# Attention with one exponential for two of four heads over a double bank, five single banks, another order of tile steps, and GpSimd's block sums in four pieces

## The chip, the core and the metric

The kernel runs on one core of a Trainium2 chip. The metric is the time of one execution on the device in microseconds (us). Below, PE is TensorE, ACT is ScalarE, DVE is VectorE, POOL is GpSimd and SP is SyncE, which issues most of the DMAs.

## The reference

x is 2048 rows by 576. The kernel computes attention with 32 heads of 18 columns on the layer norm of x and adds x, then a gated GELU block of width 4608 on the layer norm of that, and adds again:

```python
qkv = (layernorm(x) @ wqkv) ...            # q, k, v: 32 heads, 18 columns each
scores = einsum("bhqd,bhkd->bhqk", q, k) * 18 ** -0.5
p = softmax(scores, axis=-1)
h = x + (einsum("bhqk,bhkd->bhqd", p, v) ...) @ wo
g, u = layernorm(h) @ w_gate, layernorm(h) @ w_up
out = h + (gelu(g) * u) @ w_down
```

## The kernel before

The kernel has three stages: projections (to about 215 us), attention (to about 1405 us), and the gated block (to the end). The change is in attention, and in the buffers that the projections share with it.

Attention works in 32 **rounds** (n, line 1220), NS = NG x NB: eight groups of four heads, four blocks of 512 queries each. A round has 16 **key tiles** (kt) of 128 keys. In a key tile, for each of the four heads, `score` (L663) multiplies 128 keys by 512 queries into a PSUM bank, and ScalarE takes the exponential into one of four buffers `pes`. q and k stand as three stacked fp16 parts in 54 rows, and two rows more subtract the row maximum inside the product; they come from the tile `mT`. Heads 0 and 2 use partitions 0 to 63, heads 1 and 3 partitions 64 to 127. `weigh` (L673) multiplies the exponentials of the tile before with v, in two halves of 256 queries and four 32-row outputs, in fp32, into one bank `acc` (singles[3]); a column of ones gives the denominators.

The row maxima are computed ahead, one and a half rounds before they are used, by a generator `maxima` (L742): 64 units a round, each (`max_bank`, L611) a product of 128 queries by 512 keys and a VectorE reduction (L629). For one head in four a pair of units is joined: ScalarE takes a Relu of a difference ("over", L623) and VectorE adds the other product and reduces (both, L627). After the 64 units `max_finish` (L635) reduces the parts on VectorE (L638), splits the result on GpSimd (L641 to L643), turns it with a DMA (L645) and loads eight rows of the next round's Q with four DMAs (L651), in the order of the heads. It falls at key tile 8 of a round and serves the next.

PSUM has eight banks: singles[0] to [3] and quads[0] to [3]. In attention, scores and maxima take the next of seven banks in turn (`m_ring`, L1216); the eighth is `acc`. In the projections products rotate over the four quads (`p_ring`).

The order within a key tile is a string (L1217), one for even and one for odd tiles: "s" a head's score and exponential, "m" a unit of the maxima, "w" half of the weighing of the tile before, "f" filler work.

```python
STEPS = ("ssmsmmfwmsw", "mssmssmfwwm")
```

`out_block` (L686) finishes a round during the next. VectorE copies the sums out of `acc` (L692, behind the last "w" of key tile 0), SyncE spreads the denominators (L695), and, after key tile 3, GpSimd inverts them (L702 to L706) and two DMAs spread them over the rows (L710, L711). After key tile 5 GpSimd multiplies, casts and takes the difference (L715 to L717), 512 columns each, and SyncE stores the two parts into X (L730). In the last two rounds VectorE does this.

TensorE, ScalarE, VectorE and GpSimd run their instructions in the order in which the code issues them. SyncE's queue is ordered by the scheduler, and is the same list before and after. In each group's first round, SyncE also carries the loads of the next group's heads (L572, L573, L593) and of the key differences (L606, L608).

Of the kernel before, what the change touches and what calls it, by code (L numbers as in the profile page):

```python
# [12 lines left out]
F32 = mybir.dt.float32  # L13
# [5 lines left out]
P = 128  # L19
# [12 lines left out]
def tile_block(  # L32
# [41 lines left out]
    singles = [ps.tile([P, 512], F32, name=f"bank{i}") for i in range(4)]  # L74
    pairs_in = ExitStack()
    psp = pairs_in.enter_context(tc.tile_pool(name="psp", bufs=1, space=bass.MemoryType.PSUM))
    quads = [psp.tile([P, 512], F32, name=f"quad{i}") for i in range(4)]

    def ring(items):
        while True:  # L80
            yield from items

    p_ring = ring(quads)
    m_ring = ring(singles)
    

# [336 lines left out]
    def idle_products(n):  # L423

        for _ in range(n):
            nc.tensor.matmul(quads[0], id16, parts[0][:, :512], start=True, stop=True)

    def turned(t0):

        cols = slice(t0 * P, (t0 + 2) * P)  # L430
        pts = [quads[1], quads[2], next(m_ring), next(m_ring)]
        for pt, c0 in zip(pts, (0, 2, NK + 1, NK + 3)):
            for c in range(2):
                for t in range(2):
                    o = (2 * c + t) * P
                    nc.tensor.matmul(pt[:, o : o + P], parts[t0 + t][:, (c0 + c) * P : (c0 + c + 1) * P],
                                     id16, start=True, stop=True)
            copy = nc.scalar.copy if c0 < NK else nc.vector.tensor_copy
            copy(XT[:, c0 : c0 + 2, cols], pt.rearrange("p (c t) -> p c t", c=2))
        pt = next(m_ring)  # L440
        for t in range(2):
            nc.tensor.matmul(pt[:, t * P : (t + 1) * P], parts[t0 + t][:, NK * P : (NK + 1) * P],
                             id16, start=True, stop=True)
        nc.scalar.copy(XT[:, NK, cols], pt[:, : 2 * P])
# [209 lines left out]
    NPE = 4  # L654
# [5 lines left out]
    ohl = view(nat1, O0 + 12 * TB, (2, TB), F16)  # L660
    rc_dram = [dram.tile([P, TPB * 4], F32, name=f"rc{i}") for i in range(2)]

    def score(n, kt, hh):  # L663

        g, qc = divmod(n, NB)
        pS = next(m_ring)
        Q, K = sets[g % 2][hh // 2]
        r = half(hh % 2, R1 + 2)
        nc.tensor.matmul(pS[:, :TB], K[r, kt * P : (kt + 1) * P],  # L669
                         Q[r, qc * TB : (qc + 1) * TB], start=True, stop=True)  # L670
        nc.scalar.activation(pes[(2 * kt + hh // 2) % NPE][:, hh % 2], pS[:, :TB], AF.Exp, scale=ex_reg)  # L671

    def weigh(n, kt, acc):  # L673
        for q in range(2):
# [11 lines left out]
    def out_block(n, acc):  # L686

        g, qc = divmod(n, NB)  # L690
        oT = oTs[n % 2]
        (nc.scalar.copy if n >= NS - 2 else nc.vector.tensor_copy)(oT, acc[:, :TB])  # L692
        R = 4 * TB // P
        rc = small.tile([P, R], F32, tag="rc", name="rc")
        (nc.scalar if n == NS - 1 else nc.sync).dma_start(rc, oT.rearrange("(h c) q -> h c q", c=32)[:, DH].rearrange(  # L695
            "h (p q) -> h p q", q=R))
        yield
        if n < NS - NB:
            den, rc = rc, small.tile([P, R], F32, tag="rp", name="rp")
            re = small.tile([P, R], F32, tag="re", name="re")  # L700
            for c in range(0, R, 4):
                nc.gpsimd.tensor_tensor(rc[:, c : c + 4], den[:, c : c + 4],  # L702
                                        minus_one.to_broadcast([P, 4]), op=ALU.pow)
            nc.gpsimd.tensor_mul(re, den, rc)
            nc.gpsimd.tensor_scalar(re, re, -1.0, 2.0, op0=ALU.mult, op1=ALU.add)
            nc.gpsimd.tensor_mul(rc, rc, re)  # L706
        else:
            nc.vector.reciprocal(rc, rc)
        rd = rc_dram[n % 2]
        nc.sync.dma_start(rd, rc)  # L710
        nc.sync.dma_start(rcb, rd.rearrange("(h p) q -> h (p q)", h=4).unsqueeze(1)  # L711
                         .to_broadcast([4, 32, TB]))
        yield
        if n < NS - 2:
            nc.gpsimd.tensor_mul(oT, oT, rcb)  # L715
            nc.gpsimd.tensor_copy(ohl[:, 0], oT)
            nc.gpsimd.tensor_sub(ohl[:, 1], oT, ohl[:, 0])  # L717
        else:
            nc.vector.tensor_mul(oT, oT, rcb)
            (nc.scalar.copy if n == NS - 1 else nc.vector.tensor_copy)(ohl[:, 0], oT)  # L720
            nc.vector.tensor_sub(ohl[:, 1], oT, ohl[:, 0])
        sl = slice(qc * TB, (qc + 1) * TB)
        for hh in range(4):
            f, end = (4 * g + hh) * DH, (4 * g + hh + 1) * DH
            r = 32 * hh
            while f < end:
                c, p = divmod(f, P)
                k = min(end - f, P - p)
                if c < NK:
                    nc.sync.dma_start(XT[p : p + k, c : c + NK + 2 : NK + 1, sl], ohl[r : r + k])  # L730
                else:
                    other = nc.gpsimd if n >= NS - 2 else nc.sync
                    nc.sync.dma_start(XT[p : p + k, NK, sl], ohl[r : r + k, 0])
                    other.dma_start(XT[TAIL + p : TAIL + p + k, NK, sl], ohl[r : r + k, 1])
                f += k
                r += k
# [5 lines left out]
    def maxima():  # L742

        for n in range(NS):
            mx = small.tile([P, TPB, 4, NB], F32, tag="mx", name="mx")
            over, both = ("over", "both") if n else ("one", "one")
            if n:
                nc.gpsimd.memset(mx[:, :, 0, 1::2], LOWEST)
            for u in range(0, UPS, 2):
                t, k = divmod(u, NB)  # L750
                for unit in (("one", t, k, 1), (over, t, k + 1, 0), ("one", t, k + 1, 1), ("one", t, k, 2),
                             ("one", t, k, 3), (both, t, k, 0), ("one", t, k + 1, 2), ("one", t, k + 1, 3)):
                    max_bank(n, mx, *unit)
                    yield
            max_finish(n, mx)
# [458 lines left out]
        take(mxs, 3 + (i % 5 == 4))  # L1214
        take(fill, 2 + (i % 5 in (1, 3)))
    m_ring = ring(singles[:3] + quads)  # L1216
    STEPS = ("ssmsmmfwmsw", "mssmssmfwwm")  # L1217
    OUT_AT = STEPS[0].rindex("w")
    prev = None
    for n in range(NS):  # L1220
        g, qc = divmod(n, NB)
        acc = singles[3]
        late = n > NS - NB
        for kt in range(NT):
            heads = iter(range(4))
            halves = weigh(*prev) if prev is not None else iter(())
            for step_no, step in enumerate(STEPS[kt % 2]):
                if step == "s":
                    score(n, kt, next(heads))
                elif step == "m":  # L1230
                    take(mxs)
                elif step == "w":
                    take(halves)
                    if kt == 0 and step_no == OUT_AT and prev is not None:
                        ob = out_block(prev[0], prev[2])
                        next(ob)
                else:
                    if n < NS - 1 or kt < 11:
                        take(fill, 2)
                    take(side)  # L1240
            prev = (n, kt, acc)
            if n and kt in ((1 if n == NS - 1 else 3, 6) if late else (3, 5)):
                take(ob)
            if late and kt == 11:
                run(fill)
                fill = wo_block(qc - 1, m_ring)
                take(fill, qc == 3)
            if n == NS - 2 and kt == NT - 1:
                rows = rows0()
            if n * NT + kt >= (NS - 1) * NT - 1:  # L1250
                take(rows, 2)
            if g == 0 and qc == 0 and kt == NT - 1:
                run(fill)
                init_set(sets[1])
            if g + 1 < NG and kt == 2 and qc == (1 if g == 0 and NB > 1 else 0):
                load_stacks(g + 1)
                load_ends(g + 1)
            if g + 1 < NG and kt == 8 and qc == (1 if g == 0 and NB > 1 else 0):
                key_steps(g + 1)
            if n == 1 and kt == 8:  # L1260
                load_w(of, wo, nc.gpsimd)
            if n == 2 and kt == 4:
                side = prepare_wo()
            if n == NS - NB and kt == 2:
                blank_rows()
                load_matrix(w_gate, 0, nc.gpsimd)
            if n == NS - NB and kt == 8:
                side = chain(split_early(0, 0, lambda: load_matrix(w_up, 0, nc.gpsimd)), pause(2),
                             split_early(0, 1, lambda: load_matrix(w_gate, 1, nc.gpsimd)),
                             pause(2), until_ready(second))  # L1270
# [106 lines left out]
```

## Time and profile before

| | us |
|---|---|
| median of 3 runs | 2634.18 (2632.51 to 2635.2) |
| profiled execution, its own time | 2638.2 |
| its span, first to last instruction | 2636.4 |
| PE busy over the span | 2589.5 (98%) |
| DVE | 2014.7 (76%) |
| ACT | 1662.0 (63%) |
| POOL | 819.3 (31%) |
| exponentials (L671), 2048 | 655.4 + 504.8 |
| weighing products (L677), 8192 records | 608.3 |
| maximum reductions (L629), 1552 | 552.6 + 478.6 |
| granted TensorE clock, mean | 0.997 |

Busy time counts an instruction from its start to its modelled end; instructions of one engine overlap at their ends, so that an engine that is busy all the time can still start one earlier or later. The shares are means over three stages with different limits, and attention is read from its own windows. Each fp32 product of the weighing has two records. In the timelines, rows show start, length, engine, line, operation, output and input, and how many instructions are merged; in brackets stands the idle time before and what ended it. "SPq" is the time of issue of a DMA, not its landing.

### The profile page before, as it was taken

How to read it: one execution, taken by the hardware profiler on the slowest of the kernel's cores; microseconds unless marked ns; L12 is line 12 of the kernel's file. 1: busy time of each engine (PE TensorE's matmuls, PEld its weight loads, DVE VectorE, ACT ScalarE, POOL GpSimd, SP SyncE). 2: the span in 40 equal slices, each digit the busy share in tenths (PEclk: the TensorE clock that was granted, in tenths of full speed). 3: DMA queues.
4: the chain of work that ended last, by engine and by line, in shares of the span. 5: the costliest groups of instructions: out<-in, count | busy, mean ns of one | idle time of the engine just before them, and what ended most of it. 6: DMA issues, size and time to landing. Idle time of an engine off the chain costs nothing.

```text
span 2636.4 us, 53635 instructions
## 1 busy us (share of the span) xinstructions
PE 2589.5 (98%) x20765; PEld 1200.4 (46%) x20765; DVE 2014.7 (76%) x3886; ACT 1662.0 (63%) x3122; POOL 819.3 (31%) x1160
## 2 busy tenths in 40 slices
PE   8899999999999999999999999999999999999999
PEld 4443333333333333333345555555555555555555
DVE  7368999999999999999866765656565656566653
ACT  5217999999999999999775433333333333333332
POOL 4201452232323232324575432222222222222221
PEclk9999999999999999999999999999999999999999
DMA  7411110101101010101125410101010101011110
GB/s 216 98 50 54 43 43 19 42 16 31 33 16 45 16 44 16 44 18 31 29 55 126 81 39 30 34 30 34 30 34 30 33 30 33 30 32 32 31 57 36
DMA packets 169137, 114.69 MB, mean 44 GB/s; under 512 B 88504, under 2 KB 147404, under 8 KB 168882
## 3 DMA queue, kind: packets, MB, share of 16 engines
q1 hardware_dynamic: 161198, 98.47, 13.9%
q0 software_dynamic: 7552, 12.79, 1.9%
q8 instruction: 162, 2.65, 0.4%
q14 instruction: 93, 0.76, 0.1%
q10 hardware_dynamic: 132, 0.01, 0.0%
HBM read 76.51 MB, written 15.01 MB: 35 GB/s over the span
## 4 chain that ended last, share of the span: by engine, by line
PE 87%; DVE 6%; POOL 2%; DMA 2%; issue 1%; SPq 1%; ACT 1%; DVEq 0%; ACTq 0%; POOLq 0%
PE bank L677 18%; PE more L1094 14%; PE bank L1094 14%; PE bank L300 9%; PE more L300 8%; PE quad L619 7%; PE bank L619 6%; PE quad L300 4%; PE quad L669 4%; DVE mx L629 3%; PE bank L669 3%; DVE nat L692 1%; ACT WK L671 0%; DMA A<-qk_lo 0%; POOL A L249 0%
## 5 line engine op out<-in xcount | busy, mean ns | idle before, releaser
L671 ACT ACTIVATE WK<-quad 128x512 f32<-128x512 f32 x1169 | 655.4, 620 | 24.0 <-PE quad L669 18.4
L677 PE MATMUL bank<-WK,V 128*32 128x256 f32 x8192 | 608.3, 389 | 2.4 <-DVE nat L692 0.4
L629 DVE TENSOR_REDUCE mx<-quad 128x1 f32<-128x512 f32 x834 | 552.6, 684 | 13.0 <-PE quad L669 3.0
L671 ACT ACTIVATE WK<-bank 128x512 f32<-128x512 f32 x879 | 504.8, 621 | 19.6 <-PE bank L669 17.6
L629 DVE TENSOR_REDUCE mx<-bank 128x1 f32<-128x512 f32 x718 | 478.6, 684 | 40.5 <-PE bank L619 33.0
L300 PEld LDWEIGHTS <-WK 128*128 128x128 f16 x3456 | 338.0, 98 | 90.9 <-ACT WK L1105 1.7
L1094 PEld LDWEIGHTS <-W 128*128 128x128 f16 x2394 | 234.4, 98 | 282.8 <-issue 5.5
L677 PEld LDWEIGHTS bank<-WK,V 128*32 128x32 f32 x8192 | 190.3, 108 | 270.8 <-issue 204.4
L300 PE MATMUL more<-W,WK 128*128 128x288 f16 x1728 | 235.6, 286 | 2.2 <-ACT WK L1105 1.4
L300 PE MATMUL bank<-W,WK 128*128 128x288 f16 x1728 | 235.2, 286 | 0.0
L702 POOL TENSOR_TENSOR rp<-rc,minus_one 128x4 f32<-128x4 f32 x112 | 111.3, 1012 | 382.6 <-DMA rc<-nat 382.6
L1094 PE MATMUL bank<-X,W 128*128 128x512 f16 x792 | 223.8, 379 | 0.0
L1094 PE MATMUL bank<-V,W 128*128 128x512 f16 x720 | 202.4, 379 | 0.4 <-ACT tmp L1144 0.3
L965 POOL TENSOR_TENSOR A<-A 128x384 f32<-128x384 f32 x136 | 138.1, 1036 | 202.0 <-DMA A<-in_B_w_up_dram 135.7
L619 PE MATMUL quad<-W 54*128 54x512 f16 x510 | 190.5, 383 | 0.9 <-ACT WK L671 0.6
L619 PEld LDWEIGHTS <-W 54*128 54x128 f16 x1024 | 74.8, 94 | 244.3 <-issue 228.0
L1108 POOL TENSOR_TENSOR WK<-tmp,WK 128x512 f16<-128x512 f32 x73 | 87.9, 1204 | 308.7 <-ACT WK L1105 308.4
L619 PEld LDWEIGHTS <-A 54*128 54x128 f16 x1024 | 71.4, 94 | 233.9 <-issue 213.7
L619 PE MATMUL quad<-A 54*128 54x512 f16 x463 | 172.3, 384 | 0.6 <-ACT WK L671 0.6
L669 PE MATMUL quad<-A 56*128 56x512 f16 x585 | 171.5, 382 | 1.0 <-DMA A<-mT 0.6
L669 PE MATMUL quad<-W 56*128 56x512 f16 x584 | 169.6, 381 | 2.0 <-DVE mx L629 1.9
L1112 ACT COPY tmp<-more 128x512 f32<-128x512 f32 x36 | 21.0, 583 | 236.6 <-PE more L1094 198.2
(328 smaller groups left out, 4135.5 us busy)
## 6 DMA issues: line engine op xcount, KB each, us to landing
A<-in_B_w_down_dram SPq DMA_DIRECT2D x8, 1152.0 KB
nat<-rc SPq DMA_DIRECT2D x32, 256.0 KB
A<-in_B_w_gate_dram SPq DMA_DIRECT2D x64, 128.0 KB
A<-in_B_w_up_dram SPq DMA_DIRECT2D x64, 128.0 KB
qk_hi<-tmp SPq DMA_DIRECT2D x36, 128.0 KB
qk_lo<-tmp SPq DMA_DIRECT2D x36, 128.0 KB
out_dram<-nat SPq DMA_DIRECT2D x16, 288.0 KB
X<-nat SPq DMA_DIRECT2D x100, 36.0 KB
```

Of the source, the lines that this page charges most:

```text
L300: nc.tensor.matmul(dst, a, b, start=(i == 0), stop=(i == len(pairs) - 1))
L619: nc.tensor.matmul(pm[:, :TB], Q[r, q0 : q0 + P], keys, start=True, stop=True)
L629: nc.vector.tensor_reduce(dst, pm[:, :TB], axis=AX.X, op=ALU.max)
L669: nc.tensor.matmul(pS[:, :TB], K[r, kt * P : (kt + 1) * P], Q[r, qc * TB : (qc + 1) * TB], start=True, stop=True)
L671: nc.scalar.activation(pes[(2 * kt + hh // 2) % NPE][:, hh % 2], pS[:, :TB], AF.Exp, scale=ex_reg)
L677: nc.tensor.matmul(acc[32 * hh : 32 * hh + 32, qs], Vg[n // NB][:, kt * G4 + hh * VC : kt * G4 + hh * VC + 32], pes[(2 * kt + hh // 2) % N ...
L692: (nc.scalar.copy if n >= NS - 2 else nc.vector.tensor_copy)(oT, acc[:, :TB])
L702: nc.gpsimd.tensor_tensor(rc[:, c : c + 4], den[:, c : c + 4], minus_one.to_broadcast([P, 4]), op=ALU.pow)
L965: op(W8[:, d], W8[:, a], W8[:, b])
L1094: nc.tensor.matmul(bank, w, x_, start=start and i == 0, stop=i == len(mm) - 1, skip_group_check=not start)
L1108: nc.gpsimd.tensor_sub(hl[:, 2 * i + j], v, hh[:, 2 * i + j])
L1112: nc.scalar.copy(xg, g[0])
```

## The change

Four things change together.

1. PSUM: in place of four quads there are two quads and one double bank, `twin` (two banks side by side). Scores and maxima that take one bank rotate over five (three singles, two quads). The projections rotate over the two quads and the first half of `twin`.
2. `score` takes one head or two. A new step "S" puts heads 0 and 1 side by side into `twin`, and one exponential of 128 x 1024 reads both. Heads 2 and 3 keep a bank and an exponential each. A key tile thus has three exponentials for four heads, and the order of heads is 2, then 0 and 1, then 3.
3. The strings of steps and the order of the eight units in `maxima` are new.
4. The three block sums of `out_block` are cut into four pieces of 128 columns, for all rounds but the last group's; within a piece product, cast and difference follow each other.

```diff
-    quads = [psp.tile([P, 512], F32, name=f"quad{i}") for i in range(4)]
+    twin = psp.tile([P, 2, 512], F32, name="twin")
+    quads = [psp.tile([P, 512], F32, name=f"quad{i}") for i in range(2)]
...
-    p_ring = ring(quads)
+    p_ring = ring(quads + [twin[:, 0]])
...
-    def score(n, kt, hh):
+    def score(n, kt, *heads):
...
-        pS = next(m_ring)
-        Q, K = sets[g % 2][hh // 2]
-        r = half(hh % 2, R1 + 2)
-        nc.tensor.matmul(pS[:, :TB], K[r, kt * P : (kt + 1) * P],
-                         Q[r, qc * TB : (qc + 1) * TB], start=True, stop=True)
-        nc.scalar.activation(pes[(2 * kt + hh // 2) % NPE][:, hh % 2], pS[:, :TB], AF.Exp, scale=ex_reg)
+        pS = twin if len(heads) == 2 else next(m_ring)[:, None]
+        for i, hh in enumerate(heads):
+            Q, K = sets[g % 2][hh // 2]
+            r = half(hh % 2, R1 + 2)
+            nc.tensor.matmul(pS[:, i, :TB], K[r, kt * P : (kt + 1) * P],
+                             Q[r, qc * TB : (qc + 1) * TB], start=True, stop=True)
+        dst = pes[(2 * kt + heads[0] // 2) % NPE]
+        k = heads[0] % 2
+        nc.scalar.activation(dst[:, k : k + len(heads)], pS[:, :, :TB], AF.Exp, scale=ex_reg)
...
-            nc.gpsimd.tensor_mul(oT, oT, rcb)
-            nc.gpsimd.tensor_copy(ohl[:, 0], oT)
-            nc.gpsimd.tensor_sub(ohl[:, 1], oT, ohl[:, 0])
+            cuts = 4 if n < NS - NB else 1
+            for c in range(cuts):
+                cs = slice(c * TB // cuts, (c + 1) * TB // cuts)
+                nc.gpsimd.tensor_mul(oT[:, cs], oT[:, cs], rcb[:, cs])
+                nc.gpsimd.tensor_copy(ohl[:, 0, cs], oT[:, cs])
+                nc.gpsimd.tensor_sub(ohl[:, 1, cs], oT[:, cs], ohl[:, 0, cs])
...
-    STEPS = ("ssmsmmfwmsw", "mssmssmfwwm")
+    STEPS = ("smSmmfwsmw", "msSmsmfwwm")
...
-            heads = iter(range(4))
+            lone = iter((2, 3))
...
-                if step == "s":
-                    score(n, kt, next(heads))
+                if step == "S":
+                    score(n, kt, 0, 1)
+                elif step == "s":
+                    score(n, kt, next(lone))
```

The units of `maxima` are, with the head last (the same head runs in the lower half of the array if it is even, in the upper if odd): before, heads 1, 0 ("over"), 1, 2, 3, 0 ("both"), 2, 3; after, 2, 1, 0 ("over"), 2, 1, 3, 0 ("both"), 3.

TensorE in a plain round, from the weighing in an odd key tile (both halves) to the end of the first run of products in the even tile behind it; the first product is still the odd tile's last "m". Before (L669 is a score, L619 a maximum, L677 the weighing; weight loads stand ahead of each product):

```order
L677 MATMUL bank_69<-WK,V 32x256 x8
L619 LDWEIGHTS A
L619 MATMUL quad_73<-A 128x512
L669 LDWEIGHTS W
L669 MATMUL quad_74<-W 128x512
...
L669 MATMUL quad_75<-W 128x512
...
L619 MATMUL quad_76<-A 128x512
...
L669 MATMUL bank_66<-W 128x512
...
L619 MATMUL bank_67<-nat,A 128x512
```

And after, at the same place (L671 is a score, L620 a maximum, L681 the weighing):

```order
L681 MATMUL bank_69<-WK,V 32x256 x8
L620 LDWEIGHTS A
L620 MATMUL quad_74<-A 128x512
L671 LDWEIGHTS W
L671 MATMUL quad_75<-W 128x512
...
L620 MATMUL bank_66<-A 128x512
...
L671 MATMUL twin<-W 128x512
...
L671 MATMUL twin<-W 128x512
...
L620 MATMUL bank_67<-A 128x512
...
L620 MATMUL bank_68<-nat,A 128x512
```

The first score of a tile is now head 2's; the two products of the double bank follow behind a maximum, and the single banks come round after five uses.

GpSimd, from the block sums of a round to the split of the next round's maxima. Before (nat holds the sums and the denominators' inverses, m the maxima):

```order
L715 TENSOR_TENSOR nat<-nat 128x512 [waits DMAHW1_49,DVE_49]
L716 CAST nat<-nat 128x512 [waits DMAHW5_49,DMAHW4_49,DMAHW6_49,DMAHW0_49,Pool_49]
L717 TENSOR_TENSOR nat<-nat 128x512 [waits Pool_49]
L641 TENSOR_SCALAR m<-m 128x16 [waits DVE_49]
L642 CAST mm_922<-m 128x4x4 [waits Pool_49]
L643 TENSOR_TENSOR mm_922<-m,mm_922 128x4x4 [waits Pool_49]
```

After, with the lines L722 to L724 in their place and L642 to L644 behind them:

```order
L722 TENSOR_TENSOR nat<-nat 128x128 [waits DMAHW1_49,DVE_49]
L723 CAST nat<-nat 128x128 [waits DMAHW6_49,DMAHW0_49,Pool_49]
L724 TENSOR_TENSOR nat<-nat 128x128 [waits Pool_49]
L722 TENSOR_TENSOR nat<-nat 128x128
L723 CAST nat<-nat 128x128 [waits Pool_49]
L724 TENSOR_TENSOR nat<-nat 128x128 [waits Pool_49]
...
L642 TENSOR_SCALAR m<-m 128x16 [waits DVE_49]
L643 CAST mm_921<-m 128x4x4 [waits Pool_49]
```

Twelve instructions stand where three stood, each but a piece's first waiting for the one before; the split of the maxima stays behind them.

More of the change, by code (lines that the diff above doesn't have):

```diff
@@ L425, in idle_products @@
         for _ in range(n):
-            nc.tensor.matmul(quads[0], id16, parts[0][:, :512], start=True, stop=True)
+            nc.tensor.matmul(twin[:, 0], id16, parts[0][:, :512], start=True, stop=True)
     def turned(t0):
         cols = slice(t0 * P, (t0 + 2) * P)
-        pts = [quads[1], quads[2], next(m_ring), next(m_ring)]
+        pts = quads + [next(m_ring), next(m_ring)]
         for pt, c0 in zip(pts, (0, 2, NK + 1, NK + 3)):
@@ L750, in maxima @@
                 t, k = divmod(u, NB)
-                for unit in (("one", t, k, 1), (over, t, k + 1, 0), ("one", t, k + 1, 1), ("one", t, k, 2),
-                             ("one", t, k, 3), (both, t, k, 0), ("one", t, k + 1, 2), ("one", t, k + 1, 3)):
+                for unit in (("one", t, k, 2), ("one", t, k, 1), (over, t, k + 1, 0), ("one", t, k + 1, 2),
+                             ("one", t, k + 1, 1), ("one", t, k, 3), (both, t, k, 0), ("one", t, k + 1, 3)):
                     max_bank(n, mx, *unit)
```

## Prediction

> **What bounds the kernel now.** I read the windows of busy time first, cut at the starts of rounds (a round is one value of n: four heads, 512 queries, 16 key tiles), then the timelines of one engine at a time. One plain round, and a stretch near the end of attention where no maxima are left:
>
> ```profile
> 905.04:940.87 35.83, 35.75 (x388) 11.54 (x386) 35.31 (x67) 35.71 (x74) 9.26 (x16) 1.00 0.06 18
> 1382.00:1402.20 20.20, 20.20 (x200) 6.17 (x200) 16.76 (x36) 19.83 (x40) 13.98 (x15) 1.00 0.94 135
> ```
>
> The columns after the length are PE, PE weight loads, VectorE, ScalarE and GpSimd. In the plain round three engines are busy 98.5% or more, so the shares name no bound; the engine that could not go faster must be found. TensorE's timeline over two key tiles, late in one round:
>
> ```profile
> 773.53 1.07 PE L677 MATMUL bank<-WK,V 128*32 128x256 f32 x16
> 774.53 0.39 PE L619 MATMUL bank<-A 54*128 54x512 f16 x1
> ...
> 775.51 0.64 PE L677 MATMUL bank<-WK,V 128*32 128x256 f32 x8
> ...
> 777.95 0.62 PE L677 MATMUL bank<-WK,V 128*32 128x256 f32 x5
> ```
>
> From one block of 16 weighing products to the next is 777.95 - 773.53 = 4.42 us, and it is all issue: the block holds TensorE 1.00 us, the seven score and maximum products behind it 0.98 us, and so on. Each of these seven uses half of the array's rows (heads 0 and 2 the lower, 1 and 3 the upper) and two of opposite halves run together, so seven cost four slots. Eight such pairs of tiles are 35.36 us; the round takes 35.83. TensorE sets 98.7% of a round, and what all waits together can still give is 0.47 us a round.
>
> Those waits come from VectorE's two extra jobs, the copy of the sums (L692) and the last reduction of the maxima (L638), once a round each:
>
> ```profile
> 763.82 0.68 DVE L692 COPY nat<-bank 128x512 f32<-128x512 f32 x1
> 764.42 0.68 DVE L629 TENSOR_REDUCE mx<-quad 128x1 f32<-128x512 f32 x1
> ...
> 779.38 0.69 DVE L629 TENSOR_REDUCE mx<-quad 128x1 f32<-128x512 f32 x1
> 780.18 0.22 DVE L638 TENSOR_REDUCE m<-mx 128x16 f32<-128x64 f32 x1
> 780.31 0.68 DVE L629 TENSOR_REDUCE mx<-quad 128x1 f32<-128x512 f32 x1
> ```
>
> A full operation takes 0.60 from start to start (763.82 to 764.42). From 779.38 to 780.31 stand 0.93, so L638 costs 0.33. Seven full operations in a pair of tiles are 4.20, only 0.22 under TensorE's 4.42; the 0.60 and 0.33 are made up over several pairs, while TensorE waits for banks.
>
> Last, a chain that crosses GpSimd and SyncE to the next round's first scores. In round 5, GpSimd, then SyncE, then TensorE at the start of round 6:
>
> ```profile
> 424.73 1.27 POOL L715 TENSOR_TENSOR nat<-nat 128x512 f32<-128x512 f32 x1 [6.87 <-DMA nat<-rc]
> 426.06 0.61 POOL L716 CAST nat<-nat 128x512 f16<-128x512 f32 x1
> 426.75 1.17 POOL L717 TENSOR_TENSOR nat<-nat 128x512 f16<-128x512 f32 x1
> 428.00 0.26 POOL L641 TENSOR_SCALAR m<-m 128x16 f32<-128x16 f32 x1
> 428.33 0.20 POOL L642 CAST mm<-m 128x16 f16<-128x16 f32 x1
> 428.61 0.23 POOL L643 TENSOR_TENSOR mm<-m,mm 128x16 f16<-128x16 f32 x1
> ```
> ```profile
> 398.54 2.78 SPq L651 DMA_DIRECT2D W<-mT  x4
> ...
> 408.61 2.31 SPq L593 DMA_DIRECT2D nat<-qk_lo  x3
> 411.02 0.64 SPq L695 DMA_DIRECT2D rc<-nat  x1
> ...
> 427.94 3.96 SPq L730 DMA_DIRECT2D X<-nat  x5
> 432.01 1.18 SPq L645 DMA_TRANSPOSE mT<-mm  x1
> 434.30 2.69 SPq L651 DMA_DIRECT2D W<-mT  x4
> ```
> ```profile
> 437.95 0.39 PE L669 MATMUL quad<-W 56*128 56x512 f16 x1
> ```
>
> The block sums (L715 to L717) stand ahead of the maxima's split (L641 to L643) on GpSimd, and ahead of the turn and the four row loads (L645, L651) on SyncE. So the maxima of round 6 are ready only 3.65 us, counted from the first row load, before its scores.
>
> **The change part by part.**
>
> *One exponential for two heads.* Its price is not in the trace; ScalarE's slope is:
>
> ```profile
> L283 ACT ACTIVATE W<-WK,p_s_w 128x640 f16<-128x640 f32 x8 | 6.4, 826 | 0.8 <-DVE p_s_w L173 0.8
> L283 ACT ACTIVATE W<-WK,p_s_w 128x1440 f16<-128x1440 f32 x2 | 3.0, 1493 | 0.8 <-DVE p_s_w L173 0.8
> ```
>
> (1493 - 826) / 800 = 0.83 ns an element, so 512 more cost 0.43 us. In the plain round 35.71 us hold 72 to 74 instructions, 0.48 to 0.50 each; the pair costs about 0.91 in place of 0.97, and ScalarE gains about 0.06 us a tile, 1 us a round. That is covered by TensorE's 4.42 in every round with maxima: nothing. Without maxima ScalarE does set the time (40 in 20.20 us): 24 tiles by 0.05 is -1 us.
>
> *The new order.* The seven products keep their halves' counts: in the even tile (with the one before it) 1,0,0,0,1,1,0, in the odd one 1,0,0,1,1,1,0, four of one half at most, as before. Three weighing stretches a pair of tiles as before, and the copy L692 still follows the last of tile 0. TensorE's 4.42 stays.
>
> *Five single banks and one double.* Before, 16 uses go round 7 banks in 4.42 us: a bank returns after 7/16 of it, 1.93 us. Now 12 uses go round 5: 1.84 us, and the double bank must return within a tile, 2.21 us, of which its products (0.39) and exponential (about 1.0) take 1.4. So steady tiles fit; where they don't, the double products wait on TensorE, and behind them stand the tile's other maxima, for which VectorE waits. VectorE's two extra jobs find 0.09 us less cover each, and what waits on ScalarE finds more. Bounds: all waits gone, 28 rounds by -0.47 = -13 us; both jobs paid in full, 28 by (0.93 - 0.47) = +13 us. I take 0, since the two effects are nearly equal and opposite; the ends go into the range. The products ahead of attention rotate over three banks instead of four; their readers wait for TensorE, not the reverse, and I cost it at nothing, at most 2 us (a tenth of a microsecond in each of some 20 tiles).
>
> *GpSimd's block sums in four pieces.* Twelve instructions of 128 columns for three of 512, in 28 rounds. The slope from 16 to 512 columns gives the piece: the product, priced as L643 is and with L715's length, 0.23 + 112 x (1.27 - 0.23)/496 = 0.46; the cast 0.20 + 112 x (0.61 - 0.20)/496 = 0.29; the difference 0.23 + 112 x (1.17 - 0.23)/496 = 0.44. Within a piece each waits for the one before, 0.06 to 0.08 us as between L715, L716 and L717. A piece is 1.19 + 0.14, less a slight overlap, 1.29; four are 5.2 against 428.00 - 424.73 = 3.27, less the last gap 3.2. **The chain grows by 2.0 us** (between 0, if pieces run as fast as a whole, and 2.4, with gaps after each). Nothing hides it: the first X transfer waits for all pieces, and L645 and L651 are queued behind it.
>
> What the rows tolerate, from the first row load to the first score of the next round. Rounds 10, 17, 18, 22 and 25 (the second fence also has round 5, and round 17 with its first score and the one that waited):
>
> ```profile
> 577.19 2.74 SPq L651 DMA_DIRECT2D A<-mT  x4
> 830.15 2.77 SPq L651 DMA_DIRECT2D A<-mT  x4
> 866.07 2.78 SPq L651 DMA_DIRECT2D A<-mT  x4
> 1008.54 2.75 SPq L651 DMA_DIRECT2D W<-mT  x4
> 1117.65 2.78 SPq L651 DMA_DIRECT2D A<-mT  x4
> ```
> ```profile
> 402.12 0.60 PE L669 MATMUL quad<-W 56*128 56x512 f16 x2
> 581.29 0.60 PE L669 MATMUL bank<-A 56*128 56x512 f16 x2
> 832.66 0.60 PE L669 MATMUL bank<-A 56*128 56x512 f16 x2
> 834.05 0.39 PE L669 MATMUL quad<-A 56*128 56x512 f16 x1 [0.57 <-DMA A<-mT]
> 869.21 0.39 PE L669 MATMUL bank<-A 56*128 56x512 f16 x1
> 1012.54 0.39 PE L619 MATMUL bank<-W 54*128 54x512 f16 x1
> 1120.86 0.39 PE L669 MATMUL quad<-A 56*128 56x512 f16 x1
> ```
>
> The third row load (head 2) leaves 1.50 after the first; in round 25 the score that waited for it started at 1120.86, 1117.65 + 1.50 + 1.71. So 3.21 us are needed, and head 2 now stands first. Left over: round 5 has 402.12 - 398.54 - 3.21 = 0.37, round 6 has 0.44, round 10 0.89, round 18 -0.07, round 22 0.79; 17 and 25 wait already. By the same reading 9 has 1.9, 14 3.0, 21 0.8; the others have room for what comes. The delay is 2.0 in rounds 5, 9, 17, 21 and 25. In the round after each it is 4.0: SyncE's copy of the denominators (411.02) stands behind the late row loads and L593, so that chain starts 2.0 late and grows 2.0 again. Less what the round before has already shifted, the waits are 1.6, 2.3 (rounds 5, 6), 0.1, 3.1 (9, 10), 1.0 (14), 2.0, 2.1 (17, 18), 1.2, 2.3 (21, 22) and 2.0 (25): 17.7 us. A wait lets VectorE catch up: round 17 waited about 1.2 us, yet from its first score at 832.66 to 869.21 it took 36.55, 0.72 more than 35.83, so some 0.4 comes back in each of the seven new waits. 17.7 - 2.8 = **14.9 us**.
>
> [...]
>
> **Sum.** +14.9 - 1 = +13.9 us. The profiled execution took 2638.2 us (span 2636.4, 1.8 around it), 4.0 over the median of 2634.18; it becomes 2652.1, and on the median 2648.
>
> **Rivals.**
> *The split costs the chain nothing*: pieces run at the whole's rate. For: the trace has no 128-column instruction of this kind, and spans on GpSimd are rough. Against: each small instruction there shows about 0.2 us of fixed time. Then only -1 us remains: 2633, no change.
> *ScalarE was the bound after all*, and TensorE's spacing only follows it. For: 35.71 of 35.83 busy. Against: the spacing inside a weighing block and behind it is the same wherever I look. Then a round falls by the 1 us that ScalarE gains (VectorE's own 8 x 4.20 + 0.93 = 34.5 would allow it): 28 x 1 + 1 = 29 us less, and the 14.9 of the chain stay: 2634.2 - 29 + 14.9 = 2620, faster.
> *Banks run out in every tile.* If VectorE's queue is longer than the 1.84 us that five banks leave, TensorE waits in each pair of tiles: 0.15 by 8 by 28 = 34 us beside the chain, 2682. It decides once a bank's use takes over 1.84; product, reduction and hand-over take 0.39 + 0.68 + 0.1 = 1.2, so the queue may be one operation deep (1.8), no more. [...]
>
> **Chances.** Forecast 0.65, split free 0.16, ScalarE the bound 0.10, banks short 0.09. The range: 2632 (split free, a microsecond below it) to 2661 (the forecast with both of VectorE's jobs paid in full); the two outer rivals, 0.19, lie outside. A measurement of this kernel can tell about 0.2%, 5 us. Slower by more than that: 0.65 and 0.09, less 0.03 for a small chain, 0.71; within it 0.19; faster 0.10.
>
> **What would show it.** Right: twelve GpSimd rows of about 0.3 to 0.46 a round with L724 ending 2 us later after the denominators land; TensorE rows at the starts of rounds 5, 6, 10, 17, 18, 21, 22 and 25 that wait for the maxima's rows by 1 to 3 us; plain rounds (11, 12, 15, 19) within 0.1 of 35.83; ScalarE below 97% in them. Wrong: plain rounds shorter by 0.5 or more (TensorE was no floor), longer by 0.5 (banks), or no waits at round starts (the chain had room).

## The result and the profile after

The changed kernel takes 2656.15 us (median of 6 runs, 2651.62 to 2666.14) beside 2635.3 us before (6 runs, 2632.51 to 2636.93): a ratio of 1.0084 with a 95% interval of 1.0074 to 1.0094. The forecast was 2648 in a range of 2632 to 2661. The change makes the kernel slower, by 20.9 us; the forecast said 13.9.

The profiled execution is the fastest of the six, 2651.62 us (span 2649.8). I compare it with the profiled one of before, which took 2638.2, more than any of the six runs above, so that these two are only 13.4 us apart. Therefore I measure the middle of attention in **27 rounds**, from the first weighing of round 1 to that of round 28; there the stages on either side play no part. (What lies outside them is 4.9 us shorter in this execution than in that of before; over the profiled executions of all kernels here it varies from 1657 to 1665 us.) TensorE's windows for it, before and after (length, PE busy, granted clock, DMA share, GB/s):

```profile
258.35:1231.23 972.88, 967.93 (x10370) 1.00 0.12 31
```
```profile
255.31:1246.48 991.17, 972.43 (x10370) 0.99 0.12 30
```

The same 10370 records take 18.3 us longer; 4.5 of it are busy time, the rest is idle. A plain round and the last stretch, with the columns of the prediction's first fence:

```profile
627.74:663.50 35.76, 35.68 (x384) 12.86 (x385) 35.24 (x67) 35.30 (x57) 14.46 (x32) 1.00 0.13 30
1398.00:1418.20 20.20, 19.58 (x210) 6.58 (x212) 15.63 (x27) 19.77 (x31) 14.55 (x15) 1.00 0.93 128
```

A plain round is 0.07 shorter than before, so the steady state is what was forecast. The loss stands at the starts of rounds. GpSimd and SyncE in round 5, against the prediction's fences of the same place:

```profile
427.51 0.46 POOL L722 TENSOR_TENSOR nat<-nat 128x128 f32<-128x128 f32 x1 [7.54 <-DVE mx L630]
428.03 0.29 POOL L723 CAST nat<-nat 128x128 f16<-128x128 f32 x1
...
432.22 0.43 POOL L724 TENSOR_TENSOR nat<-nat 128x128 f16<-128x128 f32 x1
432.73 0.26 POOL L642 TENSOR_SCALAR m<-m 128x16 f32<-128x16 f32 x1
```
```profile
413.07 0.64 SPq L699 DMA_DIRECT2D rc<-nat  x1
...
432.68 3.96 SPq L737 DMA_DIRECT2D X<-nat  x5
436.75 1.17 SPq L646 DMA_TRANSPOSE mT<-mm  x1
439.02 2.69 SPq L652 DMA_DIRECT2D W<-mT  x4
```

From the first product to the maxima's split are now 432.73 - 427.51 = 5.22 us, before 428.00 - 424.73 = 3.27. TensorE's first scores of rounds 4, 5, 6, 9, 14, 17, 21, 22 and 25, each with its wait in brackets:

```profile
365.18 0.39 PE L671 MATMUL bank<-W 56*128 56x512 f16 x1 [2.02 <-DMA W<-mT]
403.80 0.39 PE L671 MATMUL bank<-W 56*128 56x512 f16 x1 [2.69 <-DMA W<-mT]
442.14 0.39 PE L671 MATMUL bank<-W 56*128 56x512 f16 x1 [0.95 <-DMA W<-mT]
551.24 0.39 PE L671 MATMUL bank<-A 56*128 56x512 f16 x1 [1.60 <-DMA A<-mT]
733.45 0.39 PE L671 MATMUL bank<-W 56*128 56x512 f16 x1 [1.59 <-DMA W<-mT]
843.52 0.39 PE L671 MATMUL quad<-A 56*128 56x512 f16 x1 [2.45 <-DMA A<-mT]
989.18 0.39 PE L671 MATMUL bank<-W 56*128 56x512 f16 x1 [0.75 <-DMA W<-mT]
1026.75 0.39 PE L671 MATMUL quad<-W 56*128 56x512 f16 x1 [1.64 <-DMA W<-mT]
1135.86 0.39 PE L671 MATMUL bank<-A 56*128 56x512 f16 x1 [1.60 <-DMA A<-mT]
```

Together they are 15.3 us; the view of waits of the kernel before has one wait of 0.6 for these rows. Something else was not forecast. The windows of TensorE around the wait of round 5, and the half-clock stretches after those of rounds 9 and 17:

```profile
401.11:403.80 2.69, 0.00 (x0) 1.00 0.03 6
403.80:405.20 1.40, 1.40 (x14) 1.00 0.04 8
405.20:408.62 3.42, 3.42 (x21) 0.50 0.17 34
408.62:412.03 3.41, 3.41 (x42) 1.00 0.12 27
...
551.98:555.39 3.41, 3.41 (x24) 0.50 0.07 16
...
845.52:848.94 3.42, 3.42 (x23) 0.50 0.14 32
```

The column before the last two is the granted clock. For 3.41 us it is 0.50, and TensorE gets through 21 records in place of 42. The key tile in it takes 3.96, 3.73 and 3.65 us in place of 2.44, the length of the tile behind the one wait of before: 4.0 us in all, the other large part of the 18.3. The waits (15.3 - 0.6), these tiles and 27 rounds that are 0.07 shorter (-1.9) make 16.8 of it.

### The profile page after: what moved, and what is told of

The parts are those of the page before. It is cut to its first block, busy times and chain, and to the rows that moved or that the text cites. A ratio compares the mean times of both kernels' runs of the same rounds, so it can differ in the third digit from the quotient of the medians.

```text
span 2649.8 us, 53608 instructions
## 1 busy us (share of the span) xinstructions
PE 2591.4 (98%) x20765; PEld 1240.4 (47%) x20765; DVE 2014.5 (76%) x3886; ACT 1647.5 (62%) x2610; POOL 860.4 (32%) x1412
## 3 DMA queue, kind: packets, MB, share of 16 engines
q1 hardware_dynamic: 161198, 98.47, 13.9%
## 5 line engine op out<-in xcount | busy, mean ns | idle before, releaser
L630 DVE TENSOR_REDUCE mx<-bank 128x1 f32<-128x512 f32 x965 | 631.0, 684 | 50.1 <-PE bank L620 34.5
L681 PE MATMUL bank<-WK,V 128*32 128x256 f32 x8192 | 606.2, 390 | 2.4 <-DVE nat L696 0.5
L675 ACT ACTIVATE WK<-twin 128x1024 f32<-128x1024 f32 x512 | 522.8, 1021 | 0.4 <-PE twin L671 0.3
L630 DVE TENSOR_REDUCE mx<-quad 128x1 f32<-128x512 f32 x587 | 394.7, 684 | 13.0 <-PE bank L620 3.9
L675 ACT ACTIVATE WK<-bank 128x512 f32<-128x512 f32 x613 | 366.6, 605 | 37.0 <-PE twin L671 21.9
L681 PEld LDWEIGHTS bank<-WK,V 128*32 128x32 f32 x8192 | 189.5, 108 | 277.1 <-issue 216.5
L675 ACT ACTIVATE WK<-quad 128x512 f32<-128x512 f32 x411 | 248.5, 605 | 38.7 <-PE quad L671 15.0
L620 PE MATMUL bank<-A 54*128 54x512 f16 x578 | 195.5, 384 | 3.9 <-DMA nat<-qk_hi 3.0
L620 PE MATMUL bank<-W 54*128 54x512 f16 x538 | 194.7, 383 | 0.5 <-DVE mx L630 0.5
L1119 ACT COPY tmp<-more 128x512 f32<-128x512 f32 x36 | 20.9, 582 | 238.3 <-PE more L1101 214.6
L620 PEld LDWEIGHTS <-W 54*128 54x128 f16 x1024 | 86.2, 94 | 159.5 <-issue 137.9
L620 PEld LDWEIGHTS <-A 54*128 54x128 f16 x1024 | 82.5, 94 | 162.4 <-issue 139.4
L988 ACT ACTIVATE W<-A,p_s_m 128x768 f16<-128x768 f32 (+1 forms) x78 | 78.2, 1035 | 119.9 <-DVE p_s_m L174 119.5
```

Of the source, the lines that this page charges most:

```text
L620: nc.tensor.matmul(pm[:, :TB], Q[r, q0 : q0 + P], keys, start=True, stop=True)
L630: nc.vector.tensor_reduce(dst, pm[:, :TB], axis=AX.X, op=ALU.max)
L675: nc.scalar.activation(dst[:, k : k + len(heads)], pS[:, :, :TB], AF.Exp, scale=ex_reg)
L681: nc.tensor.matmul(acc[32 * hh : 32 * hh + 32, qs], Vg[n // NB][:, kt * G4 + hh * VC : kt * G4 + hh * VC + 32], pes[(2 * kt + hh // 2) % N ...
L988: by = hi_on or (lambda dst, src, k: nc.scalar.activation(dst, src, AF.Copy, scale=k))
L1119: nc.scalar.copy(xg, g[0])
```

## The experiments

The kernels ran in three groups, with 27 to 29 runs of the kernel before beside the first and third group (medians 2633.88 and 2633.79) and 11 beside the second (2634.35). Only whole-kernel medians carry an interval; the 27 rounds are one profiled execution each. The medians of before differ by up to 1.5 us from one set of runs to another, and a difference of medians from two sets is no better than that.

| kernel | median us | ratio to before, 95% | 27 rounds us |
|---|---|---|---|
| before | 2633.8 to 2635.3 | | 972.88 |
| changed | 2656.15 | 1.0074 to 1.0094 | 991.17 |
| e1 whole sums | 2630.57 | 0.9979 to 0.9997 | 970.42 |
| e2 split alone | 2643.83 | 1.0025 to 1.0049 | 976.36 |
| e3 split behind | 2632.23 | 0.9984 to 1.0002 | 969.55 |
| e4 two exponentials | 2636.54 | 0.9998 to 1.0015 | 973.69 |
| e5 head 2 first | 2650.35 | 1.0042 to 1.0066 | 988.58 |
| e6 double first | 2645.22 | 1.0028 to 1.0053 | 981.20 |
| e7 filled waits | 2655.31 | 1.0066 to 1.0093 | 991.40 |
| e8 other queue | 2672.25 | 1.0135 to 1.0165 | 1007.40 |
| e9 whole, behind | 2631.18 | 0.9984 to 1.0002 | 969.60 |
| e10 two pieces | 2634.19 | 0.9991 to 1.0009 | 971.83 |
| e11 before, behind | 2635.74 | 1.0000 to 1.0018 | 972.23 |

My theory was the prediction's: the pieces lengthen the chain from the denominators to the maxima's rows. The first rival was that five banks and the new order start a round more slowly.

**e1: the changed kernel without the split.**

```diff
-            cuts = 4 if n < NS - NB else 1
+            cuts = 1
```

> The changed kernel with the block sums whole again (one piece of 512 columns), everything else as changed. Theory A (the loss is the longer GpSimd chain: in the changed kernel's trace TensorE waits 15.2 us in nine waits for the maxima's rows, and three windows of 3.41 us at half clock behind such waits add 4.0): those go, and what the rest of the change gives is left, 35.76 in place of 35.83 in some 25 plain rounds (-1.8) and about -1 in the last tiles: 2631 to 2634, and at most two waits for the maxima's rows (0.6 and 1.1, as before). Theory B (the starts of rounds are slower because of five single banks and the new order, the split only falls together with it): 2648 or more, with the waits still there.

Measured 2630.57, a hair under the lower end. The view of waits has one line left for the maxima's rows:

```profile
PE bank L671 <- DMA A<-mT: 0.7, 1, 0.7
```

So the pieces make the loss, and more than all of it: the rest of the change gains 0.12% (0.03 to 0.21%). Without the split the starts of rounds are as before, and theory B in this form falls.

**e2: the kernel before with the split alone.**

```diff
-            nc.gpsimd.tensor_mul(oT, oT, rcb)
-            nc.gpsimd.tensor_copy(ohl[:, 0], oT)
-            nc.gpsimd.tensor_sub(ohl[:, 1], oT, ohl[:, 0])
+            cuts = 4 if n < NS - NB else 1
...
```

> The kernel before with only the block sums cut into four pieces. Theory A: the whole loss appears, and without the 2 to 3 us that the rest of the change gives: 2652 to 2660, with eight or nine waits for the maxima's rows of 13 to 18 us together, and a window of half clock behind some of the waits over 1.5 us. Theory B: 2635 to 2637.

Both miss: 2643.83, some 10 us of loss on the median, with hardly a wait for the rows. The trace shows only 3.5 of it in the 27 rounds (976.36 against 972.88); the profiled execution of before lay above its median, and the six runs of e2 lie between 2639.57 and 2650.46, so that the 10 are a rough figure.

```profile
PE quad L669 <- DMA A<-mT: 0.7, 2, 0.4
PE bank L669 <- DMA W<-mT: 0.6, 2, 0.3
```

The split costs 10 us in the old order and 25.6 (2656.15 - 2630.57) in the new one; in the 27 rounds it is 3.5 and 20.8 (991.17 - 970.42). The two parts work together, and theory A as I had put it was wrong in saying that the split alone is the loss. In the old order heads 0, 1 and 2 begin a round in the order of the row loads, and each score waits for its own row alone (0.30 us for the second one below). TensorE in e2, at the start of round 6:

```profile
440.02 0.39 PE L669 MATMUL quad<-W 56*128 56x512 f16 x1 [0.21 <-ACT WK L671]
440.71 0.39 PE L669 MATMUL bank<-W 56*128 56x512 f16 x1 [0.30 <-DMA W<-mT]
...
441.38 0.39 PE L669 MATMUL bank<-W 56*128 56x512 f16 x1
```

Scores, and a maximum between them, fill 1.36 us (440.02 to 441.38) that in the new order stand behind one wait for head 2, whose row is loaded third. This is theory A2.

**e5: the split in the old kernel, with head 2 first.**

```diff
-            heads = iter(range(4))
+            heads = iter((2, 0, 1, 3))
```

> The kernel before with the block sums in four pieces (as in the split alone, 2643.8) and the heads of every tile in the order 2, 0, 1, 3; banks, exponentials and steps as before. Theory A2 (formed because the split alone cost only 10 us: the other half comes from the new order, which puts head 2 first, whose row load leaves third, 1.50 us behind the first, so that the 1.4 us of cover that heads 0 and 1 gave are gone): the whole loss without the change's banks and exponentials, 2652 to 2662, with eight or nine waits of 13 to 18 us together for the maxima's rows. Theory B2 (the other half comes from five banks and the double exponential, that pick up slowly behind a wait): 2642 to 2646.

2650.35: far from B2, 1.65 us under A2's lower end. The waits are there, with banks and exponentials of before:

```profile
PE bank L669 <- DMA A<-mT: 5.1, 3, 2.0
PE quad L669 <- DMA W<-mT: 5.0, 3, 2.0
```

With three smaller ones they are 12.3 us in nine waits, and the 27 rounds go from 976.36 to 988.58, most of the way to 991.17.

**e6: the changed kernel with heads 0 and 1 ahead of head 2 in key tile 0.**

```diff
-            for step_no, step in enumerate(STEPS[kt % 2]):
+            for step_no, step in enumerate("Smsmmfwsmw" if kt == 0 else STEPS[kt % 2]):
```

> The changed kernel with the double score of heads 0 and 1 ahead of head 2 in key tile 0 alone. Theory A2: heads 0 and 1 need the first two row loads and head 2 comes 0.4 to 0.7 us later, so each of nine waits is 0.5 to 0.7 us shorter, and with fewer waits long enough for the clock to halve: 2643 to 2651. Theory B2: unchanged, 2654 to 2659.

2645.22, as A2 said: 10.9 us come back through the place of one step in one tile of sixteen. The start of round 22 shows how one long wait has become three, one for each row load as it lands:

```profile
1016.92 0.39 PE L671 MATMUL twin<-W 56*128 56x512 f16 x1 [0.91 <-DMA W<-mT]
1017.63 0.37 PE L671 MATMUL twin<-W 56*128 56x512 f16 x1 [0.33 <-DMA W<-mT]
...
1018.30 0.39 PE L671 MATMUL quad<-W 56*128 56x512 f16 x1 [0.28 <-DMA W<-mT]
```

They sum to 1.52; in the changed kernel this round waited 1.64 in one piece, after earlier rounds had already waited longer.

**e3: the four pieces behind the maxima's split.**

```diff
-            if n and kt in ((1 if n == NS - 1 else 3, 6) if late else (3, 5)):
+            if n and kt in ((1 if n == NS - 1 else 3, 6) if late else (3, 9)):
```

> The changed kernel, still with four pieces, but the block sums issued after key tile 9 in place of 5, so that GpSimd splits the maxima first and SyncE turns and loads them ahead of the X transfers. Theory A: the pieces cost nothing where they stand behind the split; the chain is even 3 us shorter than before, so all waits for the maxima's rows go: 2630 to 2634. Theory B: 2648 or more. A third reading (GpSimd's extra busy time itself slows VectorE or the DMAs): 2645 or more, with plain rounds over 35.83.

2632.23, no wait for the rows. GpSimd, then SyncE, in round 5:

```profile
419.88 0.26 POOL L642 TENSOR_SCALAR m<-m 128x16 f32<-128x16 f32 x1 [7.69 <-DVE m L639]
...
420.71 0.46 POOL L722 TENSOR_TENSOR nat<-nat 128x128 f32<-128x128 f32 x1
```
```profile
420.74 1.13 SPq L646 DMA_TRANSPOSE mT<-mm  x1
423.12 2.76 SPq L652 DMA_DIRECT2D W<-mT  x4
425.98 4.01 SPq L737 DMA_DIRECT2D X<-nat  x5
```

The rows leave 16 us earlier than in the changed kernel (423.12 against 439.02, though this kernel is only 5 us ahead there). Twelve instructions cost nothing where nobody waits behind them (969.55 us in the 27 rounds, and 969.60 with three in e9). GpSimd's busy time, the third reading, is out.

**e10: two pieces.**

```diff
-            cuts = 4 if n < NS - NB else 1
+            cuts = 2 if n < NS - NB else 1
```

> The changed kernel with two pieces of 256 columns in place of four. A piece's fixed cost is (5.25 - 3.30) / 3 = 0.65 us, so the chain grows by 0.65 instead of 1.95. The chain theory with its rooms: only the rounds with the least room wait (5, 9, 17, 25, each by 0.3 to 0.7), 2632 to 2637, under a third of the 25 us that lie between one piece and four. A cost by the number of pieces without any room: a third of it, 2639.

2634.19, 3.6 above one piece; four pieces are 25.6 above it (in the 27 rounds 1.4 and 20.8). The chain's 0.65 is mostly room, its 1.95 mostly wait, so the loss is not in proportion to the pieces. Only round 25 waits by more than a quarter of a microsecond:

```profile
PE bank L671 <- DMA A<-mT: 1.1, 1, 1.1
```

**e7: idle products in four of the waits.** Theory C priced the halved clock.

```diff
+            if kt == 0 and n in (4, 5, 9, 17):
+                pd = next(m_ring)
+                for _ in range(14):
+                    nc.tensor.matmul(pd[:, :P], id16, id16, start=True, stop=True)
```

> The changed kernel with 14 idle products of 128 columns (into a bank whose content nobody reads) ahead of the first score of rounds 4, 5, 9 and 17, where TensorE waits 1.6 to 2.7 us. Theory C (a wait that leaves TensorE idle for over some 1.4 us of one 3.41 us window halves its clock for the next window, which costs 1.2 to 1.5 us a time): the three windows at half clock go while the waits end when they did, 2651 to 2654. Rival D (the slow products behind the wait come from something else, or the extra products cost as much as they save): 2655 to 2660, windows of half clock still there.

2655.31: rival D's time, with half clock behind waits that were not filled. The start of round 5, then windows of TensorE later on:

```profile
403.41 0.96 PE L1237 MATMUL bank<-id 128*128 128x128 f16 x14
404.30 0.39 PE L671 MATMUL quad<-W 56*128 56x512 f16 x1
```
```profile
400.00:405.00 5.00, 5.00 (x62) 1.00 0.04 9
876.23:878.74 2.51, 0.01 (x2) 1.00 0.01 2
...
879.15:885.98 6.83, 6.83 (x45) 0.50 0.01 1
1025.96:1028.38 2.42, 0.01 (x2) 1.00 0.01 3
1029.34:1032.75 3.41, 3.41 (x25) 0.50 0.00 0
```

In the rounds that were filled the clock stays at 1.00: round 5 shows it in the first row, and for the others it is an estimate: over the 27 rounds TensorE is busy 976.09 us, some 3.8 of it with idle products, and the rest is no more than in the changed kernel (972.43), so that the half clock of rounds 18 and 22 accounts for all of it. But only round 9 tests that: there TensorE does nothing useful for 1.8 us (0.95 of idle products and a wait of 0.83), about as in the changed kernel (1.60). Behind round 4's wait the clock was at 1.00 in the changed kernel too. In rounds 5 and 17 no wait is left behind the 0.9 us of idle products, where the changed kernel waited 2.69 and 2.45; so in this run the rows came earlier there, and the wait itself was gone. And rounds 18 and 22, which were not filled, now wait 2.5 and 2.4 us (before the filling under 0.25, and 1.64), and have 10.24 us at half clock, as much as the changed kernel had at rounds 5, 9 and 17. Counted from the first weighing of round 1, round 17 begins 7.0 us earlier than in the changed kernel and round 19 only 1.8 earlier: most of what the filling gained was lost again at round 18. SyncE, ahead of that round:

```profile
871.68 1.15 SPq L646 DMA_TRANSPOSE mT<-mm  x1
875.54 2.78 SPq L652 DMA_DIRECT2D A<-mT  x4
```

From the turn to the first row load are 3.86 us; in the changed kernel they are 2.29 at this place (875.50 to 877.79). So 1.6 of the 2.5 us come from a slower turn, and what slowed it is not shown. Whether halved clock costs time of its own is therefore not settled by this run. The runs of the changed kernel point that way: 2651.62 us at a mean clock of 0.996, 2655.07 at 0.994, 2655.34 to 2657.48 (three runs) at 0.993, 2666.14 at 0.989. But a run with longer waits would have both a lower clock and a longer time.

**e8: the denominators' copy on GpSimd's queue.**

```diff
-        (nc.scalar if n == NS - 1 else nc.sync).dma_start(rc, ...
+        (nc.scalar if n == NS - 1 else nc.gpsimd if n < NS - NB else nc.sync).dma_start(rc, ...
```

> The changed kernel with the copy of the denominators issued by GpSimd in place of SyncE. The prediction's term (in rounds 5, 9, 17 and 21 that copy stands behind late row loads on SyncE, so that those chains start late and their delay is 4.0 instead of 2.0): the copy leaves 4 to 6 us earlier in these rounds and the waits at the starts of rounds 6, 10, 18 and 22 go, 3 to 4 us together: 2650 to 2654. Rival E (the wait of the round before has already moved TensorE by as much, so the copy is not late for it): only what room there was, 2655 to 2658.

2672.25, worse than either. In its trace rounds 6, 10, 14, 18 and 22 wait less than 0.25 us, as the prediction's term would have it (10 and 18 did so in the changed kernel too), but rounds 2, 4, 5, 9, 13, 17, 21 and 25 wait 0.5 to 4.2. GpSimd in round 4, where it also issues loads for the next group's heads:

```profile
377.33 0.80 POOL L699 DMA_DIRECT2D rc<-nat  x1 [11.54 <-DVE nat L696]
...
386.09 3.97 POOL L706 TENSOR_TENSOR rp<-rc,minus_one 128x4 f32<-128x4 f32 x4
```

The copy now heads a row of thirteen DMA issues of 0.5 us and more on the engine that must invert the denominators. The copy's place on SyncE matters for the rounds behind, but this run moved a second thing, so it gives that term no price.

**e4: two exponentials over the double bank** (whole sums).

```diff
-        nc.scalar.activation(dst[:, k : k + len(heads)], pS[:, :, :TB], AF.Exp, scale=ex_reg)
+        for i in range(len(heads)):
+            nc.scalar.activation(dst[:, k + i : k + i + 1], pS[:, i : i + 1, :TB], AF.Exp, scale=ex_reg)
```

> The block sums whole and the double bank kept, but read by two exponentials of 512 columns in place of one of 1024. The prediction's reading (ScalarE is covered by TensorE wherever maxima run): 1 to 2 us above the kernel with whole sums, all of it in the last 24 tiles, and plain rounds within 0.1 of it. The rival of the prediction (ScalarE was the bound): 25 us or more above it, plain rounds 0.8 to 1.0 longer.

2636.54, some 6 us above e1 (from the two intervals, about 2 to 8). The same plain round here and in e1:

```profile
618.92:654.80 35.88, 35.81 (x385) 12.69 (x385) 35.29 (x67) 35.51 (x72) 12.96 (x23) 1.00 0.12 31
```
```profile
620.15:655.91 35.76, 35.68 (x384) 12.87 (x384) 35.23 (x67) 35.30 (x57) 12.94 (x23) 1.00 0.12 31
```

0.12 us a round, 3.3 in the 27 (973.69 - 970.42). The rival of the prediction (ScalarE the bound, 0.8 to 1.0 a round) falls; that the join is worth nothing beside maxima was too low.

**e9 and e11: whole sums behind the split, in the changed kernel and in the one before** (the edits of e1 and e3, and that of e3 alone).

> The changed kernel with whole block sums (as in the kernel with whole sums, 2630.6) that are also issued after key tile 9, behind the split of the maxima. The chain theory: the one wait that was left there (0.7 us at the start of round 25) goes and nothing else: 2629 to 2631, no wait for the maxima's rows at all, ahead of the kernel before by 0.1 to 0.2%. If the place behind the split costs something (X stored later, ahead of nothing): 2632 or more.

> The kernel before with its whole block sums issued after key tile 9. The chain theory: the two waits that it had (rounds 17 and 25, 36.64 and 36.06 in place of 35.83 in the rounds that end with them) go, some 1 us: 2632.5 to 2634, no more, since no other round waited for the maxima. So most of what the kernel with whole sums behind the split has over the kernel before would be the exponential over two banks, not the chain.

2631.18, a hair over what I gave, and 2635.74. The first has no wait for the rows and 969.60 us for the 27 rounds, the shortest but for e3's 969.55; its median cannot be told from e1's. The second has no such wait either; its 27 rounds gain 0.65 of the 1 us expected, and its median lies above what I gave. So e1, e3 and e9 are the best here, 1.7 to 3.3 us ahead of the kernel before (only e1's interval excludes no difference) and 24 to 26 ahead of the changed one; what they have over the kernel before is the exponential, not the chain.

## Why the prediction was right, and where not

**The floor** held: 35.76 against 35.83 in a plain round, TensorE busy throughout. One sign was badly chosen: ScalarE did not fall below 97% (35.30 of 35.76), since its rows overlap at their ends (an exponential of 1024 columns takes 1.02 us, and the next row starts 0.90 after it); 57 instructions do the work of 74 in the same share.

**One exponential for two heads** was forecast at nothing beside maxima and -1 us in the last 24 tiles. It is the reverse: 0.12 a round beside maxima by e4. In the last tiles a pair takes 3.99 in place of 4.05, some 0.06 of the 0.1 forecast, and the last tile gives it back (1.52 to its weighing, 0.89 before, as one exponential now ends later than the second of two did); round 31 takes 29.42 against 29.40.

**Five banks and the order of steps**, taken as 0 between -13 and +13: e4's plain rounds, with banks and order but without the join, are 0.05 longer than before, 1.4 us in 28 rounds. The choice was right.

**The pieces** cost the chain 5.22 - 3.27 = 1.95, forecast 2.0; products, casts and differences are 0.46, 0.29 and 0.43 as worked out.

**The waits** were 17.7 in the forecast and are 15.3, with the right rounds named but for rounds 4, 10 and 18:

| round | 4 | 5 | 6 | 9 | 10 | 14 | 17 | 18 | 21 | 22 | 25 |
|---|---|---|---|---|---|---|---|---|---|---|---|
| forecast | 0 | 1.6 | 2.3 | 0.1 | 3.1 | 1.0 | 2.0 | 2.1 | 1.2 | 2.3 | 2.0 |
| measured | 2.02 | 2.69 | 0.95 | 1.60 | under 0.25 | 1.59 | 2.45 | under 0.25 | 0.75 | 1.64 | 1.60 |

That the two sums come near each other is in part luck: rounds 4, 5, 9, 14 and 17 waited some 5.6 us longer than forecast, the others some 8 less. (By the prediction's own rule, 4.0 less the room and the wait of the round before, rounds 6, 10 and 22 also come to 2.0, 3.0 and 2.0, and the sum to 17.0.)

The step that failed is "The delay is 2.0 in rounds 5, 9, 17, 21 and 25", with "In the round after each it is 4.0" behind it. Counted from the first weighing of the round, the row loads leave 3.3 us later than before in round 4 (400.60 - 368.58 against 398.54 - 369.85) and 3.9 later in round 8, so rounds 5 and 9 waited longer than forecast. That wait, and the slow tile behind it, shifted the next round by more than I subtracted: in round 5 the row loads leave only 1.67 later (439.02 - 408.73 against 434.30 - 405.68), so less was left for round 6, and likewise for rounds 10 and 18.

Round 4 waits because the chain of round 3 was late by more than the pieces. There the inverses took 3.37 us from their store to their reload on SyncE, where before it was 1.45 (L710 at 343.19, L711 at 344.64):

```profile
341.00 0.36 SPq L714 DMA_DIRECT2D rc<-rp  x1
344.37 0.59 SPq L715 DMA_DIRECT2D nat<-rc  x1
```

In round 2 they took 3.01 in place of 1.43, but that alone makes no wait: in e5, where head 2 is first too, it is 2.81 in round 2 and 1.45 in round 3, and round 4 does not wait. In e7 it is 3.53 in round 3, and round 4 waits. What lengthened it was not tried.

**What comes back.** That "some 0.4 comes back in each of the seven new waits", -2.8, had the wrong sign. Where the clock stayed at 1.00, hardly anything came back: the round that ends with round 25's wait of 1.60 takes 37.66, 1.90 over a plain one, and the next 35.70, 0.06 under it. Behind three waits the key tiles with a clock of 0.50 in them took 4.0 us longer than 2.44 each. This is the mis-sized term: over the 27 rounds the split costs 991.17 - 970.42 = 20.8 us in the new order, where I had 17.7 - 2.8 = 14.9; the waits (15.3 less e1's 0.7) and 4.0 make 18.6 of it; the other 2.2 stand for the most part in the same rounds, beside the waits, and no run here explains them.

The trace shows when the clock was halved, but not by what rule. The stretches at 0.50 last 3.41 us, and those at 405.20, 551.98, 845.52 and 1367.76 start 146.78, 293.54 and 522.24 us apart, which is 43, 86 and 153 times 3.413. With windows laid at that spacing, TensorE was idle for 2.01, 1.60 and 1.41 us in those ahead of the first three. Those of rounds 25 and 22, with 1.40 and 1.33 in one window, were followed by a clock of 1.00. Nor does idle time alone draw the line: in the same trace a window with 1.64 idle (from 1309.74) was followed by 1.00 too. The prediction had no term for the clock.

**What the parts share.** The prediction put the whole loss under "GpSimd's block sums". Its reading of room (3.21 us, because "head 2 now stands first") did hold the other part, and e2, e5 and e6 show it to be the larger one: with the old order the split costs 10 us, not 25.6, and in the 27 rounds 3.5, not 20.8. From e5 to the changed kernel 5.8 us on the medians (2.6 in the 27 rounds) are left that no run here explains.

## What to carry to other kernels

A step that makes an off-path engine slower costs nothing until it eats the room of the chain that runs through it, and then up to its whole growth, and at times more, in each round that has no room left: here 0.65 us cost 3.6, and 1.95, with waits in nine of 27 rounds, cost 25.6. Before cutting work into pieces, look for what is queued behind it; issuing the same pieces behind the urgent work made them free. And when an order of consumers changes, look whether the producers still deliver in that order: the first score should be the one whose row lands first.

## What the runs showed of the hardware

Three waits of TensorE had more lost time behind them here than their own length: they left it idle for 2.01, 1.60 and 1.41 us of one 3.41 us window, the next window had a granted clock of 0.50, and the key tiles in it took 3.96, 3.73 and 3.65 us in place of 2.44, so that the longest of these waits, 2.69 us, was followed by a tile that took 1.52 longer. The share of idle time alone does not settle it: windows with 1.33, 1.40 and 1.64 idle were followed by a clock of 1.00. What decides it is open. On GpSimd a 128-column product took 0.46 us, a 256-column one 0.73 and one of 512 columns 1.27, so about 0.2 us of each is fixed (from 128 to 512 columns it grows by 2.1 ns a column, 0.27 for 128); the exponential of 1024 columns took 1.02, and started the next 0.9 later.
